# A convolution and a two-layer block: nine blocks in halves, a written-out share of the second matmul, and another order of the first instructions

## The chip, the cores and the metric

The kernel runs on one core of one Trainium2 chip. The metric is the device time of one execution in microseconds; of several runs the median is given.

## What is computed

The input x has 8 sequences of 4096 rows of 192 values. A causal convolution of 7 taps, whose weights are a softmax per head (8 heads of 24 channels), is followed by two matrix products with a leaky ReLU between them:

```python
w = np.exp(w - max(w)); w = w / (sum(w) + 1e-9)
out = np.einsum('hk,bskhg->bshg', w, x_unf)      # x_unf: 7 rows, the row itself and the 6 before it
h = out.reshape(32768, 192) @ w_in               # 192 x 2048
g = np.maximum(0.01 * h, h)
return g @ w_out                                 # 2048 x 192
```

Inputs and output are float32; the kernel calculates in bfloat16 with float32 sums.

## The kernel before

**Blocks and groups.** A block is 512 rows of two sequences at once (partitions 0 to 63 hold one sequence's channels, 64 to 127 the other's; the 192 channels are three chunks of 64). There are 32 blocks. The first NHALF = 7 are worked in two half groups of 256 rows, the other 25 as one full group each: 39 groups, a half one of 4 steps, a full one of 8.

**A step.** Each step issues two sets of the first product (`mm1`, matmuls of L400 into one of two PSUM tiles `ph`), each followed by one ScalarE activation (L407) that writes `g` as bfloat16. A set is 12 matmuls of 256 columns in a half group, 6 of 512 columns in a full one. After the two sets come so many slots of the second product (`mm2_slot`, L426): a slot is two matmuls of 192 columns on the two row halves of the array, and 32 slots finish two output subtiles of 128 rows. The slots belong to the group before: the second product always runs behind the first. How many are issued in a step is `quota`: what is open, divided by the steps of this group. So the half groups issue 16 slots a step, the first full group, which has only a half group behind it, issues 8, and all later ones 16.

**Evacuation.** When 16 slots are done, an output subtile is copied out of PSUM by `evac_o` (L473): by ScalarE for blocks under NHALF, by VectorE for the others. `seal_round` makes the next round wait for that copy.

**The convolution** of the group ahead is 21 VectorE instructions (L187, then six of L193, for each chunk), issued between the slots; in a half group they have 256 columns, in a full one 512. They read `xt`, the transposed x, which is loaded by POOL (L78), transposed by SP's queue (L93) and kept in a tile for each pair of sequences.

**The start.** Nothing is ready there, so the first 512 rows take another way. SP loads `weight` and two parts of `x_nat` (L222, L120). POOL's order is: request of the first quarter of `w_in`, upper rows (L239, `load_w_in(0, 0)`), `sel` (a memset, L252, and two selects, L254), the identity, the quarter's lower rows, then `x_rows`, the second quarter and the second half of `w_in`, `w_out` and more of x. PE first runs warm matmuls on zeros (`warm`, L282), spreads the softmax weights over the partitions (`select`, L318), transposes the first 256 rows (`transpose_first`, L149, once both halves of x_nat are cast by L133, one on ScalarE and one on VectorE), and convolves chunks 0 and 1 of the first half group itself: 28 matmuls for each (`pe_conv_jobs`, L212) with diagonal weights that ScalarE (L343) and VectorE (L335) make; ScalarE writes them to `yt` (L368). VectorE convolves chunk 2. In the first group, which has no slots, the transposes for the next rows stand after the second set of L400, and the second half of `w_in` is first used by the fifth set. Copies out of the transposes are L168.

Of the kernel before, what the change touches and what calls it, by code (L numbers as in the profile page):

```python
# [10 lines left out]
BF16 = mybir.dt.bfloat16  # L11
# [3 lines left out]
def kernel(  # L15
# [8 lines left out]
    nc = tc.nc  # L24

    B, S, D = x.shape
    H, K = weight.shape
    Din, F = moe_w_in.shape
    GRP = D // H
# [5 lines left out]
    CH = 64  # L35
    NCH = D // CH
# [4 lines left out]
    NFC = F // 128  # L41
    NB = S // ST
    NBLK = (B // 2) * NB
    NHALF = 7
    RUN = 4
    NPEC = 2

    const_pool = ctx.enter_context(tc.tile_pool(name="const", bufs=1))
# [13 lines left out]

    groups = [(b, h * HT, HT) for b in range(NHALF) for h in range(2)]
    groups += [(b, 0, ST) for b in range(NHALF, NBLK)]

# [66 lines left out]
    def cast_first(q, e, copy):  # L132
        copy(  # L133
            out=x_half[q][:, :, :, e, :],
            in_=x_nat[q][:, e, :, :].rearrange("p s (c k) -> p c s k", c=NCH),
        )
# [26 lines left out]
    def evac_first(q, *copies):  # L163
        dst = xt[0][:, :, HALO + q * HT : HALO + (q + 1) * HT].rearrange(
            "p c (s i k) -> p i s c k", s=HS, i=2
        )
        for i, t in enumerate(ptr.pop(q)):
            copies[i](out=dst[:, i], in_=t)  # L168
# [4 lines left out]
    def conv_jobs(grp, chunks=range(NCH)):  # L173
        blk, t0, T = grp
        rp, st = divmod(blk, NB)
        if blk not in yt:
            yt[blk] = yt_pool.tile([128, NCH, ST], BF16, name="yt")
        y = yt[blk]
        jobs = []
        for c in chunks:  # L180
            for k in range(K):
                a = BASE + k + st * ST + t0
                src = xt[rp][:, c, a : a + T]
                dst = y[:, c, t0 : t0 + T]
                if k == 0:
                    jobs.append(
                        lambda s=src, d=dst, c=c: nc.vector.tensor_scalar_mul(  # L187
                            d, s, wk[:, c, 0:1]
                        )
                    )  # L190
                else:
                    jobs.append(
                        lambda s=src, d=dst, c=c, k=k: nc.vector.scalar_tensor_tensor(  # L193
                            out=d, in0=s, scalar=wk[:, c, k : k + 1], in1=d,
                            op0=mybir.AluOpType.mult, op1=mybir.AluOpType.add,
                        )
                    )
        return jobs

    def pe_conv_jobs(grp, c):  # L200


        blk, t0, T = grp
        acc = psum_o.tile([128, ST], FP32, name="acc", tag="po")
        jobs = []
        for p in range(2):
            for k in range(K):
                a = BASE + k + blk * ST + t0
                for e in range(2):
                    ps = slice(e * CH, (e + 1) * CH)  # L210
                    jobs.append(
                        lambda k=k, p=p, a=a, e=e, ps=ps: nc.tensor.matmul(  # L212
                            out=acc[ps, :T], lhsT=diag[c][ps, p, k, :],
                            rhs=xt[0][ps, c, a : a + T],
                            start=(k == 0 and p == 0), stop=(k == K - 1 and p == 1),
                        )
                    )
        return jobs, lambda scale: scale(yt[blk][:, c, t0 : t0 + T], acc[:, :T], rsum[:, c, :])
# [8 lines left out]
    junk = const_pool.tile([128, 1], FP32)  # L227
    nc.vector.memset(junk, 0.0)  # L228


    pieces = (0, NFC // 4, NFC // 2, NFC)
    w_in = [
# [4 lines left out]
    def load_w_in(n, e):  # L237
        fs = slice(pieces[n] * 128, pieces[n + 1] * 128)
        nc.gpsimd.dma_start(  # L239
            out=w_in[n][e * CH : (e + 1) * CH],  # L240
            in_=moe_w_in[:, fs].rearrange("(c p) f -> p c f", p=CH),
        )
# [4 lines left out]
        return w_in[n][ps, c, a : a - f % RUN + RUN * 128 : RUN]  # L247

    load_w_in(0, 0)

    sel = const_pool.tile([H, NCH, CH], BF16, name="sel")
    nc.gpsimd.memset(sel, 1.0)  # L252
    for sign, off in ((1, 0), (-1, GRP - 1)):
        nc.gpsimd.affine_select(  # L254
            out=sel, in_=sel, compare_op=mybir.AluOpType.is_ge, fill=0.0,
            base=off, channel_multiplier=-sign * GRP,
            pattern=[[sign * CH, NCH], [sign, CH]],
        )
    ident = const_pool.tile([128, 128], BF16)
    make_identity(nc, ident)  # L260
    load_w_in(0, 1)
# [1 line left out]
    for n in (1, 2):  # L263
# [7 lines left out]
        out=w_out.rearrange("p (c i) d -> p c i d", i=RUN),  # L271
        in_=moe_w_out.rearrange("(c p i) d -> p c i d", p=128, i=RUN),
# [7 lines left out]
    def warm(n, cols=HT):  # L280
        for _ in range(n):
            nc.tensor.matmul(  # L282
                out=wa[:, 0, 0:cols], lhsT=zero[:, 0:128], rhs=zero[:, 0:cols],
                start=True, stop=True,
            )
# [5 lines left out]
        out=nmax, in_=w9[:, 0:K], axis=mybir.AxisListType.X,  # L291
# [3 lines left out]
        out=w9[:, 0:K], in_=w9[:, 0:K], func=mybir.ActivationFunctionType.Exp,  # L295
# [38 lines left out]
    def diag_wide(c, p, n):  # L334
        nc.vector.tensor_mul(  # L335
            diag[c][:, p, 0:n],
            ident2[:, None, :].to_broadcast([128, n, CH]),
            whm[:, c, p, 0:n, None].to_broadcast([128, n, CH]),
        )

    def diag_low(c, ks):
        for k in ks:
            nc.scalar.activation(  # L343
                out=diag[c][:, 1, k, :], in_=ident2,
                func=mybir.ActivationFunctionType.Copy, scale=whm[:, c, 1, k : k + 1],
            )

    diag_wide(0, 0, K)
    cast_first(0, 0, nc.scalar.copy)
    cast_first(0, 1, nc.vector.tensor_copy)  # L350
    diag_low(0, range(2))
    transpose_first(0)
    warm(3)
# [20 lines left out]
    for c in range(NPEC):  # L374
        pe_jobs, evac_y = pe_conv_jobs(groups[0], c)
        for job in pe_jobs:
            job()
        evac_y(act_scale)


    g, po, osb, seal = {}, {}, {}, None
# [84 lines left out]
    def evac_o(n):  # L466
# [4 lines left out]
        o_sb = osb[n // 2]  # L471
        copy = nc.scalar.copy if b < NHALF else nc.vector.tensor_copy
        ins = copy(out=o_sb[:, n % 2, :], in_=po.pop(n))  # L473
# [10 lines left out]
            )  # L484
        return ins

    slot, avail = 0, 0
    for i, grp in enumerate(groups):
        blk, t0, T = grp
        steps = T // 64  # L490
        if t0 == 0:
            g[blk] = g_pool.tile([128, NFC, 2, ST], BF16, name="g", tag="g")
        quota = (avail - slot) // steps

        if i == 0:
            ahead = []
        else:
            ahead = conv_jobs(groups[i + 1]) if i + 1 < len(groups) else []
        per = -(-len(ahead) // steps)
        for j in range(steps):  # L500
            for u in range(2 * j, 2 * j + 2):
                mm1(grp, u)
                if i == 0 and u == 1:
                    transpose_first(1)
                    evac_first(1, nc.vector.tensor_copy, nc.vector.tensor_copy)
                    pe_ahead, evac_y = pe_conv_jobs(groups[1], 0)
                    ahead = conv_jobs(groups[1], range(1, NCH))
                    per = len(ahead)
                if i == 0 and u in (2, 5):

                    n = len(pe_ahead) // 2
                    for job in pe_ahead[(u - 2) // 3 * n : (u + 1) // 3 * n]:
                        job()
                if i == 0 and u == 5:
                    evac_y(act_scale)
                if i == 0 and u == 6:
                    transpose_first(2)
            if i == 1 and j == 3:
                transpose_first(3)
            jobs = ahead[per * j : per * (j + 1)]  # L520
            if T == ST:


                jobs = ahead[len(ahead) * j // steps : len(ahead) * (j + 1) // steps]
                for job in jobs:
                    job()
                jobs = []
            for _ in range(quota):
                mm2_slot(slot)
                slot += 1  # L530
            if i == 0 and j == 3:
                evac_first(2, nc.vector.tensor_copy, nc.vector.tensor_copy)
            if i == 2 and j == 1:
                transpose_x(2)
            for job in jobs:
                job()
            if i == 1 and j == 3:
                evac_first(3, nc.vector.tensor_copy, nc.vector.tensor_copy)

            last_half = t0 + T == ST  # L540
            if j == steps // 4 and last_half:
                load_x(blk + 3)
            if j == steps // 2 and last_half and blk > 0:
                transpose_x(blk + 2)
        avail += 2 * T // 128 * NFC
# [36 lines left out]
```

## Time and profile before

| | |
|---|---|
| runs | 695.04, 694.43, 695.01 us, median 695.01 |
| the profiled execution | 695.04 us, its span from first to last instruction 693.3 us |
| PE busy | 686.4 us, 99% of the span |
| VectorE, ScalarE, POOL busy | 546.8, 521.5, 147.2 us |
| chain that ended last | PE 93%, VectorE 4%, ScalarE 1%, DMA 1% |
| TensorE clock as granted | 1.000 over the whole span |

Times inside the span are counted from its first instruction. PE's busy time holds matmuls that wait half-way, and slow ones: how long a step takes from the first L400 of one to the first L400 of the next says more. "x12" is a number of instructions, and a name in square brackets with an arrow is what ended the idle time before a row.

### The profile page before, as it was taken

How to read it: one execution, taken by the hardware profiler on the slowest of the kernel's cores; microseconds unless marked ns; L12 is line 12 of the kernel's file. 1: busy time of each engine (PE TensorE's matmuls, PEld its weight loads, DVE VectorE, ACT ScalarE, POOL GpSimd, SP SyncE). 2: the span in 40 equal slices, each digit the busy share in tenths (PEclk: the TensorE clock that was granted, in tenths of full speed). 3: DMA queues.
4: the chain of work that ended last, by engine and by line, in shares of the span. 5: the costliest groups of instructions: out<-in, count | busy, mean ns of one | idle time of the engine just before them, and what ended most of it. 6: DMA issues, size and time to landing. Idle time of an engine off the chain costs nothing.

```text
span 693.3 us, 26555 instructions
## 1 busy us (share of the span) xinstructions
PE 686.4 (99%) x11996; PEld 593.9 (86%) x11996; DVE 546.8 (79%) x1026; ACT 521.5 (75%) x592; POOL 147.2 (21%) x206
## 2 busy tenths in 40 slices
PE   8999999999999999999999999999999999999998
PEld 6899999997888888888888888888888888888887
DVE  5999999998778787878877878878778878787812
ACT  5888888889877777777777777777777777777771
POOL 6822201222222012222102222112222022000000
PEclk9999999999999999999999999999999999999999
DMA  9986535569466256564555665455665455232112
GB/s 147 116 96 83 83 70 75 69 93 92 59 87 86 62 81 78 74 81 83 77 74 73 80 81 82 71 81 68 85 82 74 78 74 67 70 59 59 49 41 65
DMA packets 184161, 53.82 MB, mean 78 GB/s; under 512 B 149104, under 2 KB 183664, under 8 KB 184048
## 3 DMA queue, kind: packets, MB, share of 16 engines
q0 software_dynamic: 99536, 14.76, 30.6%
q1 hardware_dynamic: 84512, 37.38, 23.0%
q8 instruction: 93, 1.52, 0.9%
q14 instruction: 20, 0.16, 0.1%
HBM read 29.88 MB, written 25.17 MB: 79 GB/s over the span
## 4 chain that ended last, share of the span: by engine, by line
PE 93%; DVE 4%; ACT 1%; DMA 1%; issue 0%; SPq 0%
PE po L426 47%; PE ph L400 45%; DVE yt L193 3%; ACT g L407 1%; PE acc L212 1%; DMA x_nat<-in_x_dram 1%; DVE yt L187 0%; DVE xt L168 0%; PE warm L282 0%; DVE x_half L133 0%; PE ptr L149 0%; ACT yt L368 0%; SPq L120 0%; SPq L222 0%; PE ptr L156 0%
## 5 line engine op out<-in xcount | busy, mean ns | idle before, releaser
L407 ACT ACTIVATE g<-ph 128x1024 bf16<-128x1024 f32 x512 | 496.3, 1021 | 148.1 <-PE ph L400 147.7
L193 DVE SCALAR_TENSOR_TENSOR yt<-xt,wk,yt 128x512 bf16<-128x512 bf16 (+1 forms) x684 | 450.3, 658 | 19.4
L426 PE MATMUL po<-w_out,g 64*128 64x192 bf16 (+1 forms) x8064 | 387.6, 243 | 0.0
L426 PEld LDWEIGHTS <-g 64*128 64x128 bf16 (+1 forms) x8064 | 360.9, 94 | 31.1 <-issue 0.2
L400 PE MATMUL ph<-yt,w_in 64*128 64x512 bf16 (+1 forms) x3744 | 384.5, 338 | 1.7 <-ACT g L407 0.7
L400 PEld LDWEIGHTS <-w_in 64*128 64x128 bf16 x3744 | 237.1, 110 | 59.0 <-issue 4.2
L78 POOL DMA_DIRECT2D x_bf<-in_x_dram x180 | 133.8, 775 | 425.1 <-DMA xt<-x_bf 422.5
L473 DVE COPY o_sb<-po 128x192 f32<-128x192 f32 x200 | 71.3, 357 | 114.0 <-PE po L426 108.1
L187 DVE TENSOR_SCALAR yt<-xt,wk 128x512 bf16<-128x512 bf16 (+1 forms) x114 | 39.7, 348 | 2.3 <-DMA xt<-x_bf 2.2
L473 ACT COPY o_sb<-po 128x192 f32<-128x192 f32 x56 | 17.9, 319 | 3.1 <-PE po L426 0.2
L212 PE MATMUL acc<-xt,diag 64*64 64x256 bf16 x84 | 7.4, 345 | 0.0
L212 PEld LDWEIGHTS <-diag 64*64 64x64 bf16 x84 | 5.7, 141 | 1.7 <-DVE wk L362 0.4
L282 PE MATMUL warm<-zero 128*128 128x256 bf16 (+1 forms) x20 | 4.8, 405 | 1.1 <-DVE junk L228 1.1
L168 DVE COPY xt<-ptr 128x384 bf16<-128x384 bf16 x7 | 2.2, 346 | 4.2 <-PE ptr L156 4.2
L127 POOL DMA_DIRECT2D x_half<-in_x_dram x6 | 4.3, 718 | 4.7 <-DMA w_in<-in_moe_w_in_dram 4.7
L282 PEld LDWEIGHTS <-zero 128*128 128x128 bf16 x20 | 2.4, 136 | 2.1 <-DVE junk L228 1.1
L239 POOL DMA_DIRECT2D w_in<-in_moe_w_in_dram x6 | 3.9, 657 | 0.8 <-POOLq L566 0.8
L343 ACT ACTIVATE diag<-ident,whm 128x64 bf16<-128x64 bf16 x14 | 3.5, 338 | 0.0
L368 ACT ACTIVATE yt<-acc,rsum 128x256 bf16<-128x256 f32 x3 | 1.4, 472 | 2.4 <-PE acc L212 2.4
L123 POOL DMA_DIRECT2D x_rows<-in_x_dram x4 | 2.9, 735 | 0.0
L168 ACT COPY xt<-ptr 128x384 bf16<-128x384 bf16 x1 | 0.5, 478 | 2.3 <-PE ptr L149 2.3
L149 PEld LDWEIGHTS <-x_half 64*128 64x128 bf16 x24 | 0.7, 107 | 1.5 <-issue 1.5
(38 smaller groups left out, 13.4 us busy)
## 6 DMA issues: line engine op xcount, KB each, us to landing
out_dram<-o_sb SPq DMA_DIRECT2D x117, 192.0 KB, 2.1
x_bf<-in_x_dram POOLq DMA_DIRECT2D x180, 64.0 KB, 3.3
out_dram<-o_sb SPq DMA_DIRECT2D x22, 96.0 KB, 1.6
xt<-x_bf SPq DMA_TRANSPOSE x90, 2.8
w_in<-in_moe_w_in_dram POOLq DMA_DIRECT2D x4, 192.0 KB, 5.5
w_in<-in_moe_w_in_dram POOLq DMA_DIRECT2D x2, 384.0 KB, 9.5
w_out<-in_moe_w_out_dram POOLq DMA_DIRECT2D x1, 768.0 KB, 12.8
x_nat<-in_x_dram SPq DMA_DIRECT2D x2, 192.0 KB, 3.3
```

The costliest lines, as they stand in the source:

```text
L78: nc.gpsimd.dma_start(out=t[:, c, :, e, :], in_=src[2 * rp + e, :, :, c * CH : (c + 1) * CH],)
L127: nc.gpsimd.dma_start(out=x_half[q][:, c, :, e, :], in_=rows[:, e, :, c * CH : (c + 1) * CH],)
L187: lambda s=src, d=dst, c=c: nc.vector.tensor_scalar_mul(d, s, wk[:, c, 0:1])
L193: lambda s=src, d=dst, c=c, k=k: nc.vector.scalar_tensor_tensor(out=d, in0=s, scalar=wk[:, c, k : k + 1], in1=d, op0=mybir.AluOpType.mult, ...
L212: lambda k=k, p=p, a=a, e=e, ps=ps: nc.tensor.matmul(out=acc[ps, :T], lhsT=diag[c][ps, p, k, :], rhs=xt[0][ps, c, a : a + T], start=(k == ...
L239: nc.gpsimd.dma_start(out=w_in[n][e * CH : (e + 1) * CH], in_=moe_w_in[:, fs].rearrange("(c p) f -> p c f", p=CH),)
L282: nc.tensor.matmul(out=wa[:, 0, 0:cols], lhsT=zero[:, 0:128], rhs=zero[:, 0:cols], start=True, stop=True,)
L343: nc.scalar.activation(out=diag[c][:, 1, k, :], in_=ident2, func=mybir.ActivationFunctionType.Copy, scale=whm[:, c, 1, k : k + 1],)
L400: nc.tensor.matmul(out=ph[:, e, i * T : (i + 1) * T], lhsT=w_in_of(f, ps, c), rhs=y[ps, c, t0 : t0 + T], start=(c == 0), stop=(c == NCH - 1),)
L407: act = nc.scalar.activation(out=g[blk][:, nf * u : nf * (u + 1), :, t0 : t0 + T], in_=ph.rearrange("p e (i t) -> p i e t", i=nf), func=my ...
L426: return nc.tensor.matmul(out=po[m], lhsT=g[b][ps, fc, e, s * 128 : (s + 1) * 128], rhs=w_out[ps, fc, :], start=start, stop=stop,)
L473: ins = copy(out=o_sb[:, n % 2, :], in_=po.pop(n))
```

## The change

Five edits. The select on POOL is issued before the tiles of `w_in` and the request of its first quarter, not after them. Both casts of x_nat are ScalarE's. Two warm matmuls stand on PE between the two chunks that it convolves. Nine blocks are in halves in place of seven: 41 groups. And for the last two half groups and the first full one the slots of each step are written out; the sums are 48, 48 and 96, where the rule would give 64, 64 and 64.

```diff
-    NHALF = 7
+    NHALF = 9
...
-    load_w_in(0, 0)
-
     sel = const_pool.tile([H, NCH, CH], BF16, name="sel")
     nc.gpsimd.memset(sel, 1.0)
     for sign, off in ((1, 0), (-1, GRP - 1)):
...
+    load_w_in(0, 0)
     ident = const_pool.tile([128, 128], BF16)
     make_identity(nc, ident)
     load_w_in(0, 1)
...
     diag_wide(0, 0, K)
-    cast_first(0, 0, nc.scalar.copy)
-    cast_first(0, 1, nc.vector.tensor_copy)
+    for e in range(2):
+        cast_first(0, e, nc.scalar.copy)
     diag_low(0, range(2))
...
         evac_y(act_scale)
+        if c == 0:
+            warm(2)
...
+    plan = {
+        2 * NHALF - 2: [16, 8, 8, 16],
+        2 * NHALF - 1: [8, 8, 16, 16],
+        2 * NHALF: [16, 8, 8, 16, 8, 8, 16, 16],
+    }
...
-        quota = (avail - slot) // steps
+        quota = plan.get(i, [(avail - slot) // steps] * steps)
...
-            for _ in range(quota):
+            for _ in range(quota[j]):
```

More of the change, by code (lines that the diff above doesn't have):

```diff
@@ L228 @@
     nc.vector.memset(junk, 0.0)
+    sel = const_pool.tile([H, NCH, CH], BF16, name="sel")
+    nc.gpsimd.memset(sel, 1.0)
+    for sign, off in ((1, 0), (-1, GRP - 1)):
+        nc.gpsimd.affine_select(
+            out=sel, in_=sel, compare_op=mybir.AluOpType.is_ge, fill=0.0,
+            base=off, channel_multiplier=-sign * GRP,
+            pattern=[[sign * CH, NCH], [sign, CH]],
+        )
     pieces = (0, NFC // 4, NFC // 2, NFC)
@@ L249 @@
     load_w_in(0, 0)
[L251 to L258, printed above, removed]
     ident = const_pool.tile([128, 128], BF16)
```

## The prediction

> **What bounds the kernel now.** I read the windows by stage first, then PE's waits, then the order of time in the three places where PE loses anything. Columns of the windows: length, then busy time of PE, PEld, DVE, ACT and POOL with their counts, the granted clock, the DMA share and GB/s.
>
> ```profile
> 0.00:24.70 24.70, 21.27 (x297) 16.14 (x298) 15.78 (x47) 16.21 (x32) 16.10 (x30) 1.00 1.01 142
> 24.70:160.71 136.01, 135.81 (x2904) 135.62 (x2901) 127.42 (x274) 116.01 (x155) 37.38 (x51) 1.00 0.63 82
> 160.71:177.42 16.71, 16.42 (x230) 11.90 (x227) 14.13 (x21) 16.07 (x21) 7.31 (x10) 1.00 1.05 98
> 177.42:676.88 499.46, 499.46 (x8409) 417.62 (x8406) 385.68 (x675) 371.08 (x385) 86.38 (x117) 1.00 0.50 73
> ```
>
> PE is busy without a gap from 177 us on, and nearly so from 24.7 to 160.7. A step of the half groups takes 2.63 us (the chain has the matmuls `po` at 46.50 and at 49.13), one of the full groups 2.615 us (178.91, 181.52, 184.14). All slack lies at the start and in the first full group (160.71 to 177.42). There the shares are 8 slots a step:
>
> ```profile
> 160.71 1.49 PE L400 MATMUL ph<-yt,w_in 64*128 64x512 bf16 x12
> 162.67 1.76 PE L400 MATMUL ph<-yt,w_in 64*128 64x512 bf16 x12
> 164.89 1.49 PE L400 MATMUL ph<-yt,w_in 64*128 64x512 bf16 x12
> 166.84 1.76 PE L400 MATMUL ph<-yt,w_in 64*128 64x512 bf16 x12
> ```
>
> The reader sees steps of 1.96 and 2.22 us in turn: PE alone needs 2.615 - 8 x 0.0825 = 1.955 us (a slot is 1.32/16 us), and every second step it waits 0.265 us inside its matmuls L400, because the activation that frees the bank pair is not done. Four such pairs lose **1.06 us**.
>
> The start, in order of time:
>
> ```profile
> 1.31 0.75 POOL L239 DMA_DIRECT2D w_in<-in_moe_w_in_dram  x1 [0.80 <-POOLq L566]
> 5.91 0.55 DVE L133 CAST x_half<-x_nat 128x384 bf16<-128x384 f32 x1 [1.22 <-DMA x_nat<-in_x_dram]
> 6.61 0.51 PE L149 MATMUL ptr<-ident,x_half 64*128 64x64 bf16 x12 [1.00 <-DVE wraw L355]
> 7.80 5.48 PE L212 MATMUL acc<-xt,diag 64*64 64x256 bf16 x56
> 45.22 1.29 PE L400 MATMUL ph<-yt,w_in 64*128 64x256 bf16 x20 [0.20 <-DVE yt L193]
> ```
>
> The second half of x_nat lands at 5.9; DVE casts it; PE, idle for 1.00 us, transposes; the convolution on PE follows. The last row is the price of the start later on: the fourth half group's first step takes 3.02 us instead of 2.63 (44.60 to 47.62), because DVE, which has no idle time from 15.6 to 160.4, is late with `yt`. DVE's start is the transposes after the second set of L400 (15.17 us).
>
> **Part 1, the request of w_in after the select.** Bytes by queue in three stretches:
>
> ```profile
> q1 hardware_dynamic: 248, 0.18, 62.6%
> q0 software_dynamic: 147, 0.15, 75.9%
> q1 hardware_dynamic: 63, 0.04, 12.6%
> q1 hardware_dynamic: 233, 0.17, 48.5%
> ```
>
> The first row is 2.2 to 3.25 us, the next two are 3.25 to 4.5, the last is 4.5 to 5.6. q1 carries x_nat, q0 the w_in quarter. x_nat's first half goes at 0.18 MB in 1.05 us; then w_in starts and x_nat's second half nearly stands for 1.25 us. Removed: one POOL issue of 0.75 us ahead of memset and select (0.25 + 0.78 us, L252, L254). Moved behind them it begins at 2.36 instead of 1.31, so its bytes, which came 1.8 us after the issue began, come at 4.1. The second half of x_nat (0.17 MB) then runs from 3.25 alone and lands near 4.4 instead of 5.9. Bounds: 4.3 and 5.9; I take 4.4, the first half's own pace. The identity and the second w_in issue stay where they are (3.10, 3.63), since the same POOL work stands ahead of them. `sel` comes 0.75 us earlier, for nothing: its matmuls wait for w9p (3.36). The first w_in quarter lands about 1 us later, near 6.6; it is used at 13.2, and even at 11 it is covered.
>
> **Part 2, both casts on ACT.** ACT casts 3.83 to 4.34 (0.51 us) and 4.4 to 4.9, then two L343 (0.58 us) to 5.5. ACT was idle 2.32 us there, so nothing is added. The transposes are then held by the warm matmuls ahead of them (4.15 + 1.46 = 5.61; the next can enter 0.2 us before that end): 5.4 instead of 6.61, **1.2 us earlier**. Evacuation and `acc` follow: 6.6 instead of 7.80. ACT's twelve L343 (2.97 us from 7.53) shift alike and end at 9.3. If x_nat does not come earlier, ACT's two L343 slip to 7.0, before ACT's copy at 7.15: still nothing.
>
> **Part 3, two warm matmuls between the chunks, and PE's rate.** The same `acc` matmul takes 417 ns up to 11.9 us and 269 ns from 12.5 on; the distance of pairs is 0.213 us (32 of them in 3.62 us from 8.22) and then 0.107, as in the 2 x 0.65 us of 24 matmuls L400. The granted clock reads 1.00 throughout, so the change of pace at R = 12.28 is seen in durations alone. Before, 28 pairs from 7.80 end at 7.80 + 28 x 0.107 + 0.498 (12.28 - 7.80) = 13.0 (trace 13.1). After, 28 pairs and the two warm ones from 6.6 end at 6.52 + 0.498 R. Where R goes, the trace does not show. Upper bound: the same 12.28, end 12.64, 0.4 us earlier. Nearest row: 12.28 is 5.67 us after PE's only long idle (to 6.61); that idle is gone, PE is then busy from 4.15 on, R = 9.82, end 11.4, **1.6 us earlier**. Lower bound: counted from 1.13, R = 6.8, held by ACT's 9.3, end 9.9. I take 9.82.
>
> The Trainium skill, "TensorE: Matmul & The Clock Gate", section "What's actually happening", says that the rate is released after a busy window of 3413 ns that runs freely and does not start with the kernel. By it one window earlier would be an estimate of 8.87 for R and 10.9 for the end; it also speaks against any fixed gain, since the point lies elsewhere in each run. The trace agrees as far as 417 and 269 ns go; it can't show the window.
>
> **What is late next.** By the view of the tile w_in, its last part (the second half, lower rows) lands 10.1 us after its issue at 7.6, at 17.7, and the fifth set of L400 (18.02) needs it: it gains 0.25 us at most. The sixth set waited 0.46 us for ACT (19.33) and can now follow at 17.8 + 0.66 = 18.46: **0.9 us** gained for the rest of the first group. DVE starts 1.6 us earlier, as the transposes need only x_rows and the first two sets. So the loss of 0.39 at 44.60 goes too. PE's gain at the start: 0.94 + 0.39 = **1.33 us**. At R = 12.28 DVE gains 0.4 to 0.5 and bounds: 0.48 us.
>
> **Part 4, the plan.** 48 + 48 + 96 slots take the place of 64 + 64 + 64, the sum is the same, and so is the number of steps of 8: two, two and four against eight. They stand in pairs again. After a step of 16, ACT's first activation starts 0.88 us into the step of 8, the second 0.92 later and ends at 2.82; PE wants that bank pair at 1.96 + 0.65 = 2.61. Same wait of 0.265. In the second step of 8 that wait lets ACT draw level, and the step of 16 has none. Four pairs, 1.06 us, as before: **saved 0**. Bounds: all of the 1.06 goes; or a wait after each step of 8, 1.06 more. The row above repeats the pair exactly, so I take 0.
>
> **Part 5, two more blocks in halves.** 16 steps of 2.63 for 16 of 2.615: **+0.24 us**. Sixteen copies of 0.32 go from DVE to ACT, which has 0.34 us idle in each half step (two activations 1.94, copy 0.32). The cover to examine is DVE:
>
> ```profile
> 125.24 0.29 DVE L187 TENSOR_SCALAR yt<-xt,wk 128x256 bf16<-128x256 bf16 x1
> 135.21 0.28 DVE L187 TENSOR_SCALAR yt<-xt,wk 128x256 bf16<-128x256 bf16 x1
> 145.18 0.54 DVE L187 TENSOR_SCALAR yt<-xt,wk 128x512 bf16<-128x512 bf16 x1
> 158.09 2.33 DVE L193 SCALAR_TENSOR_TENSOR yt<-xt,wk,yt 128x512 bf16<-128x512 bf16 x3
> 162.66 0.35 DVE L187 TENSOR_SCALAR yt<-xt,wk 128x512 bf16<-128x512 bf16 x1 [2.24 <-DMA xt<-x_bf]
> ```
>
> A half group costs DVE 9.97 us and PE 10.52, a full one 15.2 us on DVE (145.18 to 160.42). After, the first full convolution ends at 145.18 + 4 x 9.97 + 15.2 = 200.3. PE gets there at 160.71 + 2 x 10.52 + 2 x 9.47 = 200.69 (9.47 = 2 x 2.63 + 2 x 1.97 + 0.265) and needs the third chunk 0.43 later: 0.8 us to spare, as now (0.7). The start shifts both alike.
>
> **Sum.** Profiled execution 695.04 (span 693.3 and 1.74 around it); - 1.33 + 0 + 0.24 = -1.09: span 692.2, time **694.0**. The median of before, 695.01, is the same to 0.03.
>
> **Rivals.** (a) Forecast, 694.0, chance 0.48, own range 693.5 to 694.5. (b) PE's rate rises at the same moment: 695.04 - 0.48 + 0.24 = 694.8, chance 0.20. For it: 4.5 us of warm matmuls from 1.13 did not raise it. (c) More: the plan's waits go, or the second half of w_in also lands earlier (then DVE's 1.6 bounds, 0.3 more, and up to 1.06 from the waits): 692.7 to 693.6, say 693.2, chance 0.15. (d) x_nat is no earlier, the change does not do that: two warm matmuls cost 0.21 at the fast pace, the half steps 0.24: 695.5, chance 0.10. (e) Slower: DVE is late for the first full group. Place: before its first L400; price: us for us beyond 0.8. One more wait for transposes like the 2.24 us at 162.66, and half-group periods of 10.3 us (85.05 to 95.34 took that once) make 3.5, so 2.7 beyond: 696.7. To be slower by 0.2% it needs 3.3 us of lateness. Against it: block 8's transposes get one more half group of time. Chance 0.07.
>
> About 0.2% (1.4 us) is what a measurement of this kernel can tell from none. Faster by that is under 693.6: (c) and a fifth of (a), 0.25. Slower: (e), 0.07. Range 693.0 to 695.6: it leaves out (e) and the edge of (c).
>
> **What would show it.** x_nat's second landing near 4.4, `ptr` at 5.4, `acc` at 6.6; the step from 417 to 269 ns near 9.8; the fifth L400 set right behind w_in at 17.7; no wait on DVE yt near 43; steps of 1.97 and 2.24 in pairs in the last two half groups and of 1.96 and 2.22 in the full one, four waits in all. Wrong it is if `acc` starts at 7.8, if w_in lands elsewhere than 17.7, or if PE waits for yt at the first full group.

## The result and the profile after

The changed kernel takes 693.22 us (median of six runs, 692.54 to 693.87), the one before 695.02 in the same measurement (six runs, 694.43 to 696.07). The ratio is 0.9972, with a 95% interval of 0.996 to 0.9985: faster by 0.28%, 1.8 us. The profiled execution is the fastest of the six, 692.54 us with a span of 690.8; the one of before, 695.04 and 693.3. What is compared below are these two spans, 2.5 us apart, which is more than the gain of the medians.

The stages of the changed kernel, as windows (length, busy time of PE, PEld, DVE, ACT, POOL, clock, DMA share, GB/s): the start up to the first slots of the second product, the half groups under the rule, the two half groups of the plan, the first full group.

```profile
0.00:22.39 22.39, 19.82 (x298) 14.85 (x300) 15.68 (x46) 16.61 (x33) 15.10 (x29) 1.00 1.06 154
22.39:179.06 156.67, 156.67 (x3353) 156.67 (x3350) 146.66 (x330) 134.07 (x179) 42.83 (x58) 1.00 0.64 82
179.06:197.95 18.89, 18.78 (x389) 18.38 (x386) 17.64 (x28) 17.19 (x23) 4.45 (x6) 1.00 0.57 75
197.95:216.77 18.82, 18.68 (x294) 14.73 (x291) 17.06 (x26) 17.22 (x23) 6.50 (x9) 1.00 0.72 93
```

The start ends at 22.39 instead of 24.70, **2.31 us** earlier. In the second row PE is busy for the whole length; before, 0.2 us were missing there, the wait for `yt` at 45.22, which cost its step 0.39. The planned half groups take 9.44 and 9.45 us and the full one 18.82, as the forecast's steps add up (9.47; 4 x 2.615 + 2 x (1.96 + 2.22) = 18.8). So the sum is - 2.31 - 0.39 + 0.24 for the half steps = - 2.46, of 2.5.

The start in order of time, PE of the changed kernel:

```profile
5.38 0.50 PE L149 MATMUL ptr<-ident,x_half 64*128 64x64 bf16 x12
6.56 2.10 PE L212 MATMUL acc<-xt,diag 64*64 64x256 bf16 x28
8.60 0.39 PE L282 MATMUL warm<-zero 128*128 128x256 bf16 x2
8.92 1.72 PE L212 MATMUL acc<-xt,diag 64*64 64x256 bf16 x28
16.37 1.50 PE L402 MATMUL ph<-yt,w_in 64*128 64x256 bf16 x23 [0.69 <-DMA w_in<-in_moe_w_in_dram]
```

No idle time stands before the transposes. 28 matmuls `acc` take 2.10 and then 1.72 us (5.48 for 56 before): from 7.4 us on one takes 268 ns, up to 7.0 it took 417. The last row begins with the fifth set of the first product, but for its first matmul (18.02 before): it now waits 0.69 us for the last part of w_in. Its request, the last of six, goes out at 7.1 us and takes the longest of them to land, 9.2 us, so the part is there at 16.3 (7.6 + 10.1 = 17.7 before):

```profile
L248 POOL DMA_DIRECT2D w_in<-in_moe_w_in_dram x6: 626/638/754, 1.9 to 7.1; - x6
DMA to landing us min/median/max: 4.9/6.1/9.2
```

The sixth set of before, which waits for ScalarE (ACT); in the changed kernel it begins at 16.95 without a wait:

```profile
19.33 0.85 PE L400 MATMUL ph<-yt,w_in 64*128 64x256 bf16 x12 [0.46 <-ACT g L407]
```

POOL's first work:

```profile
0.80 0.25 POOL L231 MEMSET sel<- 8x192 bf16 x1 [0.29 <-POOLq L576]
1.85 0.75 POOL L248 DMA_DIRECT2D w_in<-in_moe_w_in_dram  x1
3.14 0.65 POOL L248 DMA_DIRECT2D w_in<-in_moe_w_in_dram  x1
```

The memset begins at 0.80, while the request that stood first before began only at 1.31. So the request begins at 1.85, not at 2.36, and the second one at 3.14 instead of 3.63. Bytes by queue, from 2.2 to 3.25 us (first row) and from 3.25 to 4.5:

```profile
q1 hardware_dynamic: 291, 0.21, 78.8%
q0 software_dynamic: 77, 0.08, 54.5%
q1 hardware_dynamic: 253, 0.18, 44.7%
```

x_nat (q1) moves 0.18 MB in the second stretch, where it moved 0.04 before. Its second half lands at 4.4 instead of 5.9.

### The profile page after: what moved, and what is told of

Same layout as the page of the kernel before. It is cut to its first block, busy times and chain, and to the rows that moved or that the text cites. A ratio compares the mean times of both kernels' runs of the same rounds, so it can differ in the third digit from the quotient of the medians.

```text
span 690.8 us, 26984 instructions
## 1 busy us (share of the span) xinstructions
PE 685.0 (99%) x12190; PEld 600.9 (87%) x12190; DVE 550.4 (80%) x1051; ACT 527.0 (76%) x609; POOL 147.2 (21%) x206
## 4 chain that ended last, share of the span: by engine, by line
PE 96%; DMA 1%; ACT 1%; POOL 1%; issue 0%; DVE 0%; POOLq 0%
PE po L428 49%; PE ph L402 47%; DMA w_in<-in_moe_w_in_dram 1%; ACT g L409 1%; POOL w_in L248 0%; POOL x_rows L123 0%; PE acc L212 0%; POOL sel L233 0%; DVE o_sb L475 0%; PE ptr L156 0%; POOL ident masks.py:199 0%; POOL sel L231 0%; POOL ident masks.py:197 0%; PE ptr L149 0%; POOLq masks.py:199 0%
## 5 line engine op out<-in xcount | busy, mean ns | idle before, releaser
L193 DVE SCALAR_TENSOR_TENSOR yt<-xt,wk,yt 128x512 bf16<-128x512 bf16 (+1 forms) x720 | 458.3, 637 | 21.1
L402 PEld LDWEIGHTS <-w_in 64*128 64x128 bf16 x3936 | 246.1, 111 | 53.7 <-issue 3.0
L475 DVE COPY o_sb<-po 128x192 f32<-128x192 f32 x184 | 65.7, 357 | 109.4 <-PE po L428 100.6
L475 ACT COPY o_sb<-po 128x192 f32<-128x192 f32 x72 | 23.0, 319 | 3.9 <-PE po L428 0.2
L212 PE MATMUL acc<-xt,diag 64*64 64x256 bf16 x84 | 5.7, 283 | 0.0
```

Source lines behind the costliest of these rows:

```text
L212: lambda k=k, p=p, a=a, e=e, ps=ps: nc.tensor.matmul(out=acc[ps, :T], lhsT=diag[c][ps, p, k, :], rhs=xt[0][ps, c, a : a + T], start=(k == ...
L402: nc.tensor.matmul(out=ph[:, e, i * T : (i + 1) * T], lhsT=w_in_of(f, ps, c), rhs=y[ps, c, t0 : t0 + T], start=(c == 0), stop=(c == NCH - 1),)
```

## The experiments

**Theory A**: the gain is the start's alone; the later request lets x_nat land early, PE isn't idle, its pace rises earlier, and the landing of w_in's last part is the next bound; the plan saves nothing. **Rival B**: casts, warm matmuls or the plan carry a good part of it. From the profile after came **D**: that POOL's requests all moved ahead by 0.5 us is itself a good part. The median of before was 695.36 beside e1 to e4, 694.97 beside e5 to e8, 695.13 beside e9 to e11, 694.97 beside e12. In the table "pace" is the start of the first `acc` matmul under 300 ns, "w_in" the landing of its last part, "slots" the first slot of the second product; us, one profile each; e10 and e11 ran once.

| kernel | acc starts | pace | w_in | slots | span | median | ratio [95%] |
|---|---|---|---|---|---|---|---|
| before | 7.80 | 12.5 | 17.7 | 24.70 | 693.3 | 695.02 | |
| changed | 6.56 | 7.4 | 16.3 | 22.39 | 690.8 | 693.22 | 0.9972 [0.996, 0.9985] |
| e1 request only | 6.76 | 8.0 | 17.5 | 23.52 | 691.7 | 693.44 | 0.9964 [0.995, 0.9978] |
| e2 plan only | 7.93 | 12.8 | 17.8 | 24.92 | 693.8 | 695.32 | 0.9995 [0.9985, 1.0005] |
| e3 start only | 6.60 | 9.4 | 16.8 | 23.03 | 691.3 | 692.95 | 0.9954 [0.9938, 0.9971] |
| e4 split slots | 6.04 | at most 6.0 | 16.8 | 22.82 | 690.7 | 693.07 | 0.996 [0.9946, 0.9975] |
| e5 filled idle | 7.73 | 7.9 | 17.9 | 23.99 | 692.2 | 695.1 | 1.0003 [0.9991, 1.0016] |
| e6 half first | 6.56 | 9.3 | see below | 22.99 | 691.5 | 694.12 | 0.9982 [0.997, 0.9993] |
| e7 casts, warm | 7.77 | 10.1 | 18.0 | 24.09 | 692.4 | 694.73 | 1.0 [0.9989, 1.0012] |
| e8 e4 and e6 | 6.56 | 10.0 | see below | 23.15 | 691.0 | 692.68 | 0.9968 [0.9958, 0.9979] |
| e9 POOL late | 6.56 | 7.4 | 18.3 | 24.41 | 693.2 | 694.34 | 0.9987 [0.9978, 0.9996] |
| e10 e5 again | 8.07 | 8.2 | 17.2 | 23.22 | 692.0 | 693.7 | |
| e11 before again | 7.84 | 11.7 | 17.2 | 24.38 | 692.7 | 695.52 | |
| e12 POOL early, split | 6.24 | at most 6.2 | 16.1 | 22.19 | 690.0 | 692.82 | 0.9968 [0.9956, 0.9979] |

**e1, the request alone.**

```diff
-    load_w_in(0, 0)
     sel = ...; memset; two affine_select
+    load_w_in(0, 0)
     ident = ...
```

> The kernel before with one edit: the first quarter of w_in is requested after the select. Theory A (the whole gain is the start, and the start's gain is this request, which lets the second half of x_nat land early): x_nat's second half lands near 4.4 us, transposes on PE at 5.4, acc at 6.6, PE's rate changes before 10 us, no wait for yt at the fourth half group; time 1.5 to 2.7 us under before (the spread is the landing of the second half of w_in, 16.3 or 17.7). Theory B (casts, warm matmuls or the plan carry a good part of it): at most 0.9 us under before.

1.9 us under before at the medians, within A's range and twice B's bound. x_nat landed at 4.4, `acc` began at 6.76, and no wait for `yt` came at the fourth half group. The request carries the gain.

**e2, the plan alone** (nine halves and the written-out shares, start as before), and **e3, the start alone** (changed kernel with NHALF = 7 and an empty plan).

> The kernel before with nine blocks in halves and the written-out shares, and the start as it was. Theory A: four pairs of steps of 1.97 and 2.22 us remain, 0.24 us are added by sixteen half steps: 0.0 to 0.4 us over before. Theory B: the plan saves the waits for the activations, 0.8 to 1.1 us under before.

> The changed kernel with seven blocks in halves and the shares by the rule: only its start is left of the change. Theory A: 0.24 us under the changed kernel, 1.8 to 2.7 under before; first slots of the second product near 22.4 us; the first full group takes 16.7 us as before. Theory B: 0.8 us or more over the changed kernel.

e2: 0.9995, no difference, its four waits in the trace (steps of 1.97 and 2.22 us). e3: 692.95, 0.27 under the changed kernel's median; that agrees with the 0.24 of the half steps, but is less than the measurement tells, and first slots came at 23.0, not near 22.4, with the later pace of 9.4. B is out for the plan. The rows of the changed kernel's first full group, beside which those of before (1.96, 2.22 in turn) may be laid:

```profile
200.57 1.49 PE L402 MATMUL ph<-yt,w_in 64*128 64x512 bf16 x12
202.53 1.76 PE L402 MATMUL ph<-yt,w_in 64*128 64x512 bf16 x12
204.75 1.49 PE L402 MATMUL ph<-yt,w_in 64*128 64x512 bf16 x12
```

**e4, slots split between the sets.**

```diff
+            split = i in plan and (quota[j] == 8 or (j and quota[j - 1] == 8))
             for u in range(2 * j, 2 * j + 2):
                 mm1(grp, u)
+                # with split: half of quota[j] behind the first set, the rest behind the second
```

> The changed kernel; in the three groups with a written-out share, in each step of 8 slots and in each step right behind one, half of the slots are issued between the two sets of the first product. Theory A (the wait comes from two sets standing close together in front of two PSUM tiles, so that the second activation ends 0.26 us after PE wants its tile): evenly spread sets let ACT keep up, the four waits of 0.26 go, 1.0 us under the changed kernel (2.8 to 3.5 under before). Theory C (the three groups are bound by ACT's load, so the order does not matter): the same as the changed kernel within 0.3 us. If the copies between the rounds come too late, PE waits inside the slots instead and part of the 1.0 comes back.

PE's rows of e4 in the first full group:

```profile
200.72 0.81 PE L402 MATMUL ph<-yt,w_in 64*128 64x512 bf16 x6
201.69 0.81 PE L402 MATMUL ph<-yt,w_in 64*128 64x512 bf16 x6
202.67 0.81 PE L402 MATMUL ph<-yt,w_in 64*128 64x512 bf16 x6
203.65 0.81 PE L402 MATMUL ph<-yt,w_in 64*128 64x512 bf16 x6
```

A set every 0.98 us and no wait in front of one: the waits come from two sets close together, not from ACT's load. By the medians alone C's bound of 0.3 us would be met; it is the steps that put C out. The three planned groups take 37.10 us (179.48 to 216.58) instead of 37.71. That is 0.6 of the expected 1.0: the slots at 189.54 and 208.07 begin 0.2 us late, 0.05 us after ScalarE's copy between the rounds (189.18 and 207.71, 0.31 us each), which stood behind an activation; these two give 0.4 back. The medians of e4 and of the changed kernel, 693.07 and 693.22, can't tell that much, and the 2.8 to 3.5 us under before that were expected came out as 2.3.

**e5, the idle filled**: `warm(6)` ahead of the first transposes becomes `warm(10)`, in the kernel before. **e10** is the same again, run once.

> The kernel before with ten warm matmuls in place of six ahead of the first transposes, nothing else: x_nat's second half still lands near 5.9 us, but PE has no idle of 1 us before it. Theory A1 (what the early landing brings is chiefly that PE isn't idle, so that its matmuls change from 417 to 269 ns earlier): the change of pace comes before 10 us instead of at 12.3 to 12.8, acc begins at 7.8 as before and ends near 11 instead of 13; then the second half of w_in is late next: 0.9 to 2.2 us under before. Theory A2 (the 1.2 us by which the transposes move are the gain): within 0.3 us of before.

> e5 once more, for a second profile: the change of pace early again (under 10 us), acc at 7.7. If e5's times, no better than before, come from the landing of w_in, the last part lands at 18 us or later and PE waits for it for 1.5 us or more; if from the pace, the change of pace is later than e5's 7.95.

Both profiles show the change of pace at about 8 us, with x_nat as late as before, and spans 1.1 and 1.3 us shorter than before's 693.3: A1's mechanism. (In e10 0.42 us of the idle were left.) The times don't: 695.1, ratio 1.0003, as A2 had it. But e5's profiled execution is the fastest of its twelve (693.93), and e10's 693.7 is faster still, so the profiles don't show the typical one: the twelve spans have a median of 693.4. Neither sign that was set for e10 came clearly (last part of w_in at 17.2 with a wait of 0.8 us, pace at 8.2), so why e5 is no faster stays open. An earlier pace alone is not shown to bring time. e10's shows one way in which a gain is lost, DVE and then PE:

```profile
161.33 0.35 DVE L187 TENSOR_SCALAR yt<-xt,wk 128x512 bf16<-128x512 bf16 x1 [3.66 <-DMA xt<-x_bf]
```

```profile
176.48 1.06 PE L400 MATMUL ph<-yt,w_in 64*128 64x512 bf16 x8 [0.30 <-DVE yt L193]
```

With seven halves the second full group begins a new tile of `xt`; DVE waits for its transposes at 161, and the step at 175.5 takes 3.12 us instead of 2.62. Of eight profiles with seven halves two show this (e9, e10), of six with nine halves none.

**e6, the second half of w_in requested ahead of the second quarter**, sets of the first group in the order 0, 1, 4, 5, 6, 7, 2, 3, else the changed kernel. **e8** adds e4's split.

> The changed kernel, with the second half of w_in requested ahead of the second quarter, and the first group's sets in the order 0, 1, 4, 5, 6, 7, 2, 3. Theory A (after the change the landing of w_in's last part, 16.3 to 17.5 us, is what PE waits for in the first group): no wait for w_in is left, the first slots of the second product come 0.5 to 1.2 us earlier than the changed kernel's 22.4 to 22.8, time 0.5 to 1.2 us under it. Rival (ACT or the transposes for the next rows are as late): within 0.3 us of the changed kernel.

> Both: the second half of w_in first, and in the planned groups the slots of a step of 8, and of the step behind one, split between the two sets. By theory A the two gains add: 0.6 us from the split (its trace showed 18.62 and 18.48 us in place of 18.89 and 18.82) and 0.5 to 1.2 from w_in: 1.1 to 1.8 us under the changed kernel, 3 to 4 under before.

The wait for w_in is gone in both (the half lands at 13.6 to 14.0, the quarter at 16.0 to 16.1). But the sixth set then waits 0.46 us for ACT, as before the change, and the slots begin at 22.99 and 23.15. Both expectations failed (e8, at 692.68, is 0.5 us under the changed kernel and 2.3 under before, not 1.1 to 1.8 and 3 to 4): with the pace changing at 9.3 ACT is the bound, not w_in; e3, with w_in in the old order and 9.4, began at 23.03. e6's time (694.12) is even above that of the changed kernel, and this stays open, as e8 has nearly the same start and 692.68; e6's profile, the fastest of its twelve runs, does not show its typical one. The spans of e6 and e8 differ by 0.6, as the split has it.

**e7, both casts on ACT and the two warm matmuls**, request as before.

> The kernel before with both casts on ACT and two warm matmuls between the chunks, the request of w_in where it was. Theory A (these two edits bring nothing of themselves): x_nat's second half lands at 5.9, PE idle 1 us before the transposes, change of pace at 12.3 or later; 0.0 to 0.3 us over before. Theory B (they are needed for the gain): 0.5 us or more under before.

Ratio 1.0: neither a gain nor a cost. x_nat landed at 6.0, PE was idle for 0.97 us, the pace changed at 10.1, earlier than I had set. B is out here too.

**e9, POOL late**: e1 with two memsets of a spare tile on POOL behind the request.

> As e1 (request after the select, nothing else of the change), with two POOL memsets of a spare tile behind the request, so that the identity and all later requests of POOL are issued as late as in the kernel before (identity ready at 3.7 instead of 3.2, last request of w_in at 7.6 instead of 7.1). Theory A (x_nat's early landing makes the gain): x_nat still lands at 4.4, acc at 6.6 to 6.8; 1.2 to 2.0 us under before. Theory D (POOL's half microsecond, won because the select fills a time in which the first request would have to wait anyway, makes a good part, through the last part of w_in): at most 0.9 us under before, and the last part of w_in lands at 17.7 or later again.

This run bears most on where the surplus over the forecast came from. The first row is POOL's second request of w_in in e9 (3.63 before, 3.14 in the changed kernel); the others are PE's waits:

```profile
3.56 0.65 POOL L239 DMA_DIRECT2D w_in<-in_moe_w_in_dram  x1
```

```profile
12.98 0.30 PE L402 MATMUL ph<-yt,w_in 64*128 64x256 bf16 x1 [0.56 <-DMA w_in<-in_moe_w_in_dram]
14.23 0.84 PE L402 MATMUL ph<-yt,w_in 64*128 64x256 bf16 x11 [0.95 <-DMA w_in<-in_moe_w_in_dram]
18.39 1.50 PE L402 MATMUL ph<-yt,w_in 64*128 64x256 bf16 x23 [1.31 <-DMA w_in<-in_moe_w_in_dram]
```

`acc` begins at 6.56 and the pace changes at 7.4, just as in the changed kernel. Yet PE waits 2.8 us for w_in, whose last part lands at 18.3, and the slots begin at 24.41. Time: 0.8 us under before, against 1.9 for e1. So of e1's 1.9 some 0.8 is what x_nat and PE's pace bring alone, and some 1.1 hangs on POOL's 0.4 us. The intervals of the two ratios (0.995 to 0.9978, 0.9978 to 0.9996) touch, and they come from two measurements; the order is shown, the size of each part is rough. e9's profiled execution (694.88) is also 0.5 us above its median, and holds the wait at the second full group that e10 has, so its 24.41 need not be typical.

**e11, the kernel before again.**

> The kernel before once more, for a second profile: PE idle 1 us ahead of the transposes, change of pace anywhere between 10 and 13.4, last part of w_in between 17.5 and 18.5 us; the first slots of the second product between 24.0 and 25.0.

As expected but for w_in, 17.2 (I had 17.5 to 18.5).

**e12, e4 with the memsets of sel and identity on VectorE.**

> e4 (the changed kernel with split slots), and the memsets of sel and of the identity on VectorE instead of POOL, so that all of POOL's requests move ahead by 0.2 to 0.4 us more. Theory D (the time of POOL's requests, through the last part of w_in, is a good part of the gain): the last request of w_in at 6.7 to 6.9 instead of 7.1, its landing at 15.9 to 16.7, first slots of the second product at 22.0 to 22.7, time 0.2 to 0.8 us under e4's 693.07 (2.3 to 3.0 us under before). Theory A alone (only x_nat and PE's pace count): the same as e4 within 0.2 us, or worse if the first request now meets x_nat's second half.

Last request at 6.87, landing at 16.1, slots at 22.19, as D had them. The time does not decide: 692.82 is 0.25 us under e4, but 2.15 under the before of its own measurement, where e4 was 2.29 under its own and D asked for 2.3 to 3.0. The profiled span of 690.0, the shortest of all, is that of the fastest of seven runs.

## Why the prediction was right, and where it missed

The time lay in the range: 694.0 was forecast, with 693.0 to 695.6, and 693.22 measured; it is faster, as forecast, by more. Yet one of its own signs of being wrong came: w_in's last part did not land at 17.7. The likeliest case's own range (693.5 to 694.5) was missed too. The time came out where rival (c) put it, 693.2, but that is luck: of (c)'s two reasons the plan's waits did not go, and for the other, w_in landing earlier, (c) had 0.3 us, which gives 693.7.

- **x_nat.** Landing 4.4, transposes 5.4, `acc` 6.6: measured 4.4, 5.38, 6.56.
- **PE's pace.** Taken at 9.82, it changed at 7.4, between the bounds of 6.8 and 12.28. Other kernels without the idle show at most 6.0 (e4), under the lower bound, up to 10.0. The end of `acc` was set 1.6 us earlier and came 2.6 earlier.
- **The failed step** is this sentence: "The identity and the second w_in issue stay where they are (3.10, 3.63), since the same POOL work stands ahead of them." They came at 2.60 and 3.14, 0.5 us earlier. The row of before that I quoted said why, in its bracket: the first request had waited until 1.31 for POOL's queue, a time that a memset needs not wait out. With it fell "at 17.7" for w_in's last part: 16.3. The fifth set thus gained 1.65 us, not 0.25, and the sixth, free of ACT's wait, 2.4. **The mis-sized term is the first group's 0.94: it measured 2.31.** Part of that is the execution that was profiled: over the four profiles with these request times and the old order of w_in's parts (changed, e1, e3, e4) the slots begin at 22.94 on average, over the three with the start of before (before, e2, e11) at 24.67. That is 1.73, still nearly twice 0.94; in e1, where w_in's last part landed at 17.45, it was 1.18. e9 speaks for POOL's requests as the reason: the same early `acc`, with the later requests put back, loses more than half of e1's gain.
- **The wait for yt at the fourth half group**, 0.39: gone, as forecast. But it was no steady cost of the kernel before: e2, with the same start, lost 0.10 us at that step (2.73 us), and e11, the kernel before itself, nothing. Its step there, up to the next one at 46.92, takes 2.63 us:

```profile
44.29 1.50 PE L400 MATMUL ph<-yt,w_in 64*128 64x256 bf16 x24
```

- **The plan.** Saved 0, shown by the four pairs in the trace and by e2. (The forecast's working of the wait, 2.82 against 2.61, gives 0.21, not the 0.265 of the row; 0.25 to 0.26 was measured.)
- **Half steps**, + 0.24: the steps are 2.63 us as said; e3's 0.27 agrees, without proof.
- **DVE at the first full group.** It ended at 197.55 with PE there at 197.95 and in need of the third chunk at 198.4: 0.8 to spare, as worked out. (e) did not come.

That the median gain (1.8) is less than the profile's (2.5) is the spread of the runs: single times of one kernel lie 1.2 to 4.2 us apart, and the profile after shows the shortest of six spans (690.8 to 692.1, median 691.55). With 1.73 for the start, nothing for the wait and 0.24 lost in the half steps the sum is a gain of 1.5, nearer to the medians' 1.8.

## What to carry to other kernels

When work is moved ahead of a waiting instruction, look at what ended that instruction's wait: moved work that needs not wait for it fills a gap, and everything behind comes earlier, not later. In a start, follow each transfer on its own queue in stretches of a microsecond: a large request that nobody needs soon can push aside the small one that the whole chain hangs on. And where two buffers stand between two engines, the spacing of the sets that fill them counts: with the same work, e4's even spacing took four waits away (0.6 us of its three groups, in the trace).

## What the runs showed of the hardware

- **PE's pace rises late, at another point in each run, and later where PE had been idle.** In the four profiles with the idle of 1 us (before, e2, e7, e11) it changed 5.9, 6.0, 3.5 and 5.0 us after the idle's end. The Trainium skill, "TensorE: Matmul & The Clock Gate", section "What's actually happening", has a busy window of 3413 ns that runs freely; by it an estimate of 3.4 to 6.8 us (one window to two) follows, and the four lie in it. The views read 1.00 for the granted clock throughout, but where a trace keeps a record of the clock (12 of 14 do), the first one, of full clock, begins only where the pace changes: at 12.41 us in before, 7.39 in the changed kernel, 4.73 in e4, 4.95 in e12. For the time ahead of it the views' 1.00 is no reading. Without an idle of 1 us these records begin at 4.73 to 9.71 us (eight profiles), with it at 10.01 to 12.72 (four). They last 682.67 or 686.08 us, 200 or 201 times 3.413, so a window of that length can be seen in them.
- **A DMA request on POOL began no earlier than 1.31 us where it stood first, a memset in its place at 0.80.**
- **One queue's transfer can hold back another's**: beside w_in's bytes x_nat moved 0.04 MB in 1.25 us, 0.18 MB in the same stretch when w_in's came later.
- **Half a microsecond in POOL's requests moved the landing of w_in's last part by about one, on average**: with the last request at 7.5 to 7.6 it landed at 17.2 to 18.3 (seven profiles, mean 17.7), at 7.1 with the same order at 16.3 to 17.5 (four, mean 16.8). The two ranges overlap, and why the shift is larger than that of the requests stays open.
